# Two layers of convolution and feed-forward with their gradients: w1's gradient made features by rows, in pairs of blocks, with column halves

## The chip, the cores and the metric

One core of one Trainium2 chip. The metric is device time of one launch in microseconds (us), the median of several runs; lower is better. A profile belongs to one execution, whose own time is given beside it. PE is the matrix engine (TensorE), PEld its weight loads, ACT, DVE and POOL are ScalarE, VectorE and GpSimd, and SP is the engine whose queue here only starts DMAs. A matmul multiplies weights that lie in the 128x128 array (`lhsT`, at most 128 rows by 128 columns) by a moving operand (`rhs`, 128 rows by up to 512 columns) and adds into PSUM: one partition for each column of the weights, one column for each column of the moving operand.

## The reference

The forward function is applied to a sequence of 2048 tokens with D = 448 features, and the reference returns its output and the gradients of all inputs and weights but one:

```python
x = A_q
x = x + _A_ref(_layernorm(x), A_k, A_v, A_shift_k, A_ssm_k, A_ssm_D)
x = x + _B_ref(_layernorm(x), B_w1, B_w2)
x = x + _A_ref(_layernorm(x), A_k, A_v, A_shift_k, A_ssm_k, A_ssm_D)
x = x + _B_ref(_layernorm(x), B_w1, B_w2)
```

`_A_ref` is a gated long convolution through an FFT. `_B_ref` is the feed-forward part, with F = 1792:

```python
h = jnp.einsum("bsd,df->bsf", x, w1)
h = _silu(h)
out = jnp.einsum("bsf,fd->bsd", h, w2)
```

Output 7 is the gradient of w1, shape (448, 1792), bfloat16. For each of the two uses of `_B_ref` it is the sum over all tokens of (normalised row of x) times (gradient at h), and the two are added. Output 8, w2's gradient, is a sum of the same kind, shape (1792, 448).

## The kernel before

Tokens lie in 16 tiles of 128 (`NT`), features of the feed-forward part in 14 blocks of 128 (`NF`). The kernel has three stages. A prefix computes spectra and convolutions. `Main.run` goes over four chunks of 512 tokens, forward and backward through both layers; it stores the activations `a` and the gradients `g` at h to device memory (`OP_d`), laid out so that a block of 128 features of all tokens can be loaded as a tile [128 tokens, 16, 128 features] of 512 KB. `_ssm_suffix` then computes the gradients of the convolution.

The gradients of w2 and w1 are made by the class `Jobs`. `Jobs.steps` is a generator that issues the matmuls in order; it stops at each `yield`, and the code around it takes up a few steps with `jobs.run(n)`. The order of TensorE's instructions is the program's (`manual_schedule`), so the jobs' matmuls stand in TensorE's queue exactly where they are woven in: from the last chunk of `Main.run` on, all through the suffix, and what is left at the very end (`jobs.run(1000)`, L1352). One step is four matmuls of 448 columns.

For w1, a call of `group` (L1005) makes one block `f` of 128 features (the last call makes two, 12 and 13). It loads the block's tile of `g` of layer 1 (`load`, L972), takes a PSUM bank (`bank`, L998), and issues 16 matmuls (`mms`, L992), one for each tile of tokens. Then it does the same with layer 0 into the same bank. The weights are `g`'s tile and the moving operand is the normalised row (`n3` for layer 1, `n1` for layer 0, all 448 features), so the sum stands as [128 features of h, 448 features of x], the transpose of what is stored:

```python
self.nc.tensor.matmul(ps[:, :D], lhsT=st[:, t, :], rhs=mov[:, t, :],
                      start=(first and t == 0), stop=(last and t == NT - 1))
```

`fin_w1` (L1102) copies the bank to a tile `dout` on ACT and leaves it pending. The next call of `fin_w1` or `fin_w2` calls `flush` (L1108): four TensorE transposes of 112 features each into the bank `tr` (`ps_dt`, L1117), a copy on ACT to the tile `do7` (L1119), and a DMA from POOL's queue to output 7 (L1120). w2's blocks have their sum as it is stored and need no transposes: `fin_w2` (L1095).

`load` takes its tiles in turn from two pools with three buffers each. All loads go through SP's queue in their order. `bank` takes its tags in turn from po, jb, po; po has two banks, jb and tr one each. `n1` and `go2` (L1079, L1072) load a moving operand at the first call: `n1` over the tile of `go`, `go2` over the tile of `n3`, so each waits until the operand before it has been read.

Elsewhere the kernel uses parts of the array at once. In `_products` (L513) the last 64 of the 448 rows of two blocks lie on the array's upper and lower 64 rows, and their matmuls stand side by side. In the suffix, L1318 multiplies bands of 32 features on four (at the end two) groups of 32 columns, with 128 moving columns:

```python
nc.tensor.matmul(pd[32 * b:32 * b + 32, 0, P * r0:P * r0 + P], lhsT=gks[:, sl_, ch],
                 rhs=kx[:, sl_:sl_ + 4, ch], start=(sl_ == 0), stop=(sl_ == 15))
```

L235 and L236 (inverse transforms) and L1305 are full matmuls of 128 moving columns, each with weights of its own.

Of the kernel before, what the change touches and what calls it, by code (L numbers as in the profile page):

```python
# [11 lines left out]
BF16 = mybir.dt.bfloat16  # L12
# [5 lines left out]
P = 128  # L18
S = 2048
D = 448  # L20
F = 1792
J = 16
NT = 16
DC = 112
ND = 4
NF = 14
# [60 lines left out]
class _Bal:  # L87

    def __init__(self, nc):
        self.nc = nc  # L90
        self.load = {"act": 0.0, "dve": 0.0}
# [446 lines left out]
class Main:  # L538
# [245 lines left out]
    def run(self, es):  # L784
# [27 lines left out]
        def steps(pattern, **gens):  # L812
            for ch in pattern:
                next(gens[ch], None)

        steps("GGtttG", G=g20, t=self.T2(self.n0[0][1], nT))
        gb = gb_load(0)
        weave("H" * 7, H=self.H(0, 0, nT, r, range(14)))
# [7 lines left out]
        gh21 = []  # L826
        g21 = self.G(gT, gh21)
        steps("GGGG", G=g20)
        next(g20, None)
        nT = self.nT()  # L830
        steps("tGtGtGt", G=g21, t=self.T2(self.n1[1], nT))
        r = []
        weave("H" * 7, H=self.H(0, 1, nT, r, (1, 3, 5, 6, 7, 9, 11, 13)))
# [89 lines left out]
class Jobs:  # L923


    def __init__(self, k, main):
        self.k, self.nc, self.main = k, k.nc, main
        self.pool = main.ch
        self.n_ld = self.n_bank = 0
        self.pend = None  # L930
        self.last_ld = None

    def gen(self):
# [71 lines left out]
    def group(self, fts, keys, movs, fin, tags=None):  # L1005
        ps = {}
        tags = tags or [None] * len(fts)
        for i, ft in enumerate(fts):
            st = self.load(keys[0], ft)
            ps[ft] = self.bank(tags[i])  # L1010
            yield from self.mms(ps[ft], st, movs[0](), 0, NT, True, False)
        if fts == (12, 13):
            self.go2()
        for ft in fts:
            st = self.load(keys[1], ft)
            if fts == (5, 6) and ft == 5:
                self.load_n3()
            yield from self.mms(ps[ft], st, movs[1](), 0, NT, False, True)
            fin(ft, ps[ft])
# [17 lines left out]
    def steps(self):  # L1037
        g2 = lambda: self.k.mov2
        go = lambda: self.go
        keys = (("a", 1), ("a", 0))  # L1040
        yield from self.opening()
        yield from self.group((3,), keys, (go, g2), self.fin_w2, tags=("jb",))
        yield from self.group((4,), keys, (go, g2), self.fin_w2, tags=("tr",))
        yield from self.group((5, 6), keys, (go, g2), self.fin_w2)
        wkeys = (("g", 1), ("g", 0))
        movs = (lambda: self.n3, self.n1)
        for f in range(12):
            yield from self.group((f,), wkeys, movs, self.fin_w1)
        yield from self.group((12, 13), wkeys, movs, self.fin_w1)
        for f in range(7, 13):  # L1050
            yield from self.group((f,), keys[::-1], (g2, self.go2), self.fin_w2)
        yield from self.last_block(keys[::-1], (g2, self.go2))

    def last_block(self, keys, movs):

        nc, k = self.nc, self.k
        ft = NF - 1
        o = self.out()
        st = [self.load(key, ft) for key in keys]
        for lo, hi in ((0, 320), (320, D)):  # L1060
            ps = self.bank(None)
            for i in range(2):
                mov = movs[i]()
                for t in range(NT):
                    nc.tensor.matmul(ps[:, lo:hi], lhsT=st[i][:, t, :], rhs=mov[:, t, lo:hi], start=(i == 0 and t == 0), stop=(i == 1 and t == NT - 1))  # L1065
                    if t % 4 == 3:
                        yield 1
            nc.scalar.copy(o[:, lo:hi], ps[:, lo:hi])
            nc.sync.dma_start(out=k.outs[8][ft * P:(ft + 1) * P, lo:hi], in_=o[:, lo:hi])
        self.flush()  # L1070

    def go2(self):  # L1072
        k = self.k
# [21 lines left out]
    def fin_w2(self, ft, ps):  # L1095
        nc, k = self.nc, self.k
        o = self.out()
        nc.scalar.copy(o[:], ps[:, :D])
        self.flush()
        (nc.gpsimd if ft < NF - 2 else nc.sync).dma_start(out=k.outs[8][ft * P:(ft + 1) * P, :], in_=o[:])  # L1100

    def fin_w1(self, ft, ps):  # L1102
        o = self.out()
        self.nc.scalar.copy(o[:], ps[:, :D])
        self.flush()
        self.pend = (ft, o)

    def flush(self):  # L1108
        nc, k = self.nc, self.k
        if self.pend is None:  # L1110
            return
        ft, o = self.pend
        self.pend = None
        out7v = k.outs[7].rearrange("(c p) f -> p c f", p=DC)
        pt = k.psum.tile([DC, ND, P], BF16, name="ps_dt", tag="tr", bufs=1)
        for dc in range(ND):
            nc.tensor.transpose(pt[:, dc, :], o[:, dc * DC:(dc + 1) * DC], k.ident[:])  # L1117
        o7 = k.dp3.tile([DC, ND, P], BF16, name="do7", tag="do7", bufs=2)
        nc.scalar.copy(o7[:], pt[:])  # L1119
        nc.gpsimd.dma_start(out=out7v[:, :, ft * P:(ft + 1) * P], in_=o7[:])  # L1120


class APart:
# [259 lines left out]
```

## Time and profile before

| | |
|---|---|
| time, median of 3 runs | 717.25 us (716.99 to 719.49) |
| time of the profiled execution | 716.31 us |
| its span, first to last instruction | 714.5 us |
| mean granted TensorE clock | 0.995 |
| w1's matmuls (`ps_d<-n3m` and `ps_d<-n1m`) | 448, from 531.9 to 662.8 us |
| w1's transposes (`ps_dt`) | 56, from 549.3 to 672.7 us |
| ACT's copies of w1's sums (L1104), of the transposes (L1119) | 14 of 537 ns, 14 of 601 ns |
| POOL's issues to output 7 (L1120) | 14 of 730 ns |
| landing of a tile `dstat` after its issue | 3.5 to 15.3 us, median 5.7 us |

A line of a group of instructions reads: line of the program, engine, operation, output<-inputs, shapes, count | busy time (the union of the spans) and mean span of one in ns | idle time of the engine before them. A matmul's span includes the time that its results take to leave the array, so spans of a stream of matmuls overlap, and the cost of one is the distance from its start to the next one's. In the chain of waits, each piece is start, length and work; it runs backwards from the last instruction over what released each.

### The profile page before, as it was taken

How to read it: one execution, taken by the hardware profiler on the slowest of the kernel's cores; microseconds unless marked ns; L12 is line 12 of the kernel's file. 1: busy time of each engine (PE TensorE's matmuls, PEld its weight loads, DVE VectorE, ACT ScalarE, POOL GpSimd, SP SyncE). 2: the span in 40 equal slices, each digit the busy share in tenths (PEclk: the TensorE clock that was granted, in tenths of full speed). 3: DMA queues.
4: the chain of work that ended last, by engine and by line, in shares of the span. 5: the costliest groups of instructions: out<-in, count | busy, mean ns of one | idle time of the engine just before them, and what ended most of it. 6: DMA issues, size and time to landing. Idle time of an engine off the chain costs nothing.

```text
span 714.5 us, 12786 instructions
## 1 busy us (share of the span) xinstructions
PE 689.3 (96%) x5008; PEld 380.9 (53%) x5008; DVE 486.2 (68%) x1106; ACT 444.2 (62%) x582; POOL 123.3 (17%) x208
## 2 busy tenths in 40 slices
PE   6997899999999999999999999999999999999998
PEld 4886654434444444444444444544566666656655
DVE  4788776758887747877279723934258769869790
ACT  3878877686777868778677685132755555545200
POOL 1034420111011100111001100001212223353130
PEclk9999899999999999999999999999999999999999
DMA  9949998659969999499975999089999897879962
GB/s 303 305 146 234 342 287 255 168 139 270 236 146 235 215 240 242 116 243 231 224 179 133 233 229 365 3 187 249 309 413 357 291 343 245 266 274 377 354 181 95
DMA packets 196237, 172.59 MB, mean 242 GB/s; under 512 B 143090, under 2 KB 174194, under 8 KB 195024
## 3 DMA queue, kind: packets, MB, share of 16 engines
q1 hardware_dynamic: 181280, 115.30, 61.3%
q0 software_dynamic: 13344, 52.54, 20.9%
q10 hardware_dynamic: 1552, 3.94, 1.5%
q8 instruction: 39, 0.64, 0.4%
q14 instruction: 22, 0.18, 0.1%
HBM read 73.25 MB, written 60.10 MB: 187 GB/s over the span
## 4 chain that ended last, share of the span: by engine, by line
PE 62%; issue 8%; DVE 5%; ACT 4%; DMA 3%; POOL 2%; POOLq 0%; DVEq 0%; ACTq 0%
PE ps_d L995 12%; PE ps_n L741 12%; PE ps_h L513 11%; PE ps_g L513 10%; PE ps_o L695 7%; PE ps_d L1030 3%; ACT dT L688 2%; DMA ksf<-KS_d 1%; PE ps_t L580 1%; PE ps_gK L1305 1%; PE ps_tr L1211 1%; POOL rstd L279 1%; PE ps_d L1065 1%; PE ps_s L206 1%; DVE n L287 1%
## 5 line engine op out<-in xcount | busy, mean ns | idle before, releaser
L995 PEld LDWEIGHTS <-dstat 128*128 128x128 bf16 x768 | 72.5, 98 | 61.1
L513 PE MATMUL ps_h<-nT,w1sb 128*128 128x512 bf16 (+1 forms) x448 | 97.4, 380 | 2.6 <-ACT dT L678 1.9
L741 PE MATMUL ps_n<-w1T,ghT 128*128 128x448 bf16 x448 | 92.5, 353 | 0.8 <-DVE ghT L866 0.8
L695 PE MATMUL ps_o<-w2sb,aT 128*128 128x448 bf16 x448 | 88.5, 352 | 0.0
L513 PE MATMUL ps_g<-nT,w2T 128*128 128x512 bf16 (+1 forms) x392 | 82.9, 380 | 0.1
L723 ACT CAST ghT<-ps_g 128x512 bf16<-128x512 f32 (+1 forms) x74 | 54.1, 760 | 41.5 <-PE ps_g L513 41.2
L673 ACT ACTIVATE aT<-ps_h 128x512 bf16<-128x512 f32 (+1 forms) x82 | 60.0, 759 | 29.2 <-PE ps_h L513 27.6
L513 PEld LDWEIGHTS <-w1sb 128*128 128x128 bf16 (+1 forms) x448 | 35.5, 97 | 59.7 <-issue 25.4
L741 PEld LDWEIGHTS <-ghT 128*128 128x128 bf16 x448 | 43.2, 98 | 42.3 <-DVE ghT L866 1.7
L695 PEld LDWEIGHTS <-aT 128*128 128x128 bf16 x448 | 43.5, 98 | 40.1
L513 PEld LDWEIGHTS <-w2T 128*128 128x128 bf16 (+1 forms) x448 | 35.4, 97 | 55.1 <-issue 20.8
L915 DVE SCALAR_TENSOR_TENSOR lb_v<-lb_u,n 128x448 bf16<-128x448 bf16 x48 | 30.0, 624 | 46.8 <-ACT lb_u L745 46.3
L279 POOL TENSOR_TENSOR rstd<-ln_ve,mhalf 128x2 f32<-128x2 f32 (+2 forms) x27 | 23.0, 851 | 198.8 <-DVE ln_ve L277 198.8
L688 ACT ACTIVATE dT<-dT 128x1024 bf16<-128x1024 bf16 (+1 forms) x64 | 55.0, 940 | 0.1
L995 PE MATMUL ps_d<-n1m,dstat 128*128 128x448 bf16 x224 | 48.6, 352 | 0.0
L995 PE MATMUL ps_d<-n3m,dstat 128*128 128x448 bf16 x224 | 48.6, 352 | 0.0
L678 ACT CAST dT<-ps_h 128x1024 bf16<-128x1024 f32 (+1 forms) x50 | 42.8, 872 | 0.0
L745 ACT ACTIVATE lb_u<-ps_n,rstd 128x448 bf16<-128x448 f32 x32 | 20.7, 647 | 34.5 <-PE ps_n L741 26.3
L995 PE MATMUL ps_d<-X,dstat 128*128 128x448 bf16 x160 | 34.2, 353 | 0.0
L995 PE MATMUL ps_d<-go,dstat 128*128 128x448 bf16 x160 | 33.7, 353 | 0.0
L581 ACT COPY nT<-ps_t 128x1024 bf16<-128x1024 bf16 x20 | 20.2, 1008 | 18.7 <-PE ps_t L580 18.7
L866 DVE TENSOR_TENSOR ghT<-dT,ghT 128x512 bf16<-128x512 bf16 (+2 forms) x24 | 18.1, 778 | 19.2 <-ACT ghT L723 17.0
(217 smaller groups left out, 1245.1 us busy)
## 6 DMA issues: line engine op xcount, KB each, us to landing
dstat<-g_d SPq DMA_DIRECT2D x28, 512.0 KB, 5.6
dstat<-a_d SPq DMA_DIRECT2D x23, 512.0 KB, 7.1
a_d<-turned SPq DMA_DIRECT2D x16, 512.0 KB, 4.1
g_d<-turned SPq DMA_DIRECT2D x16, 512.0 KB, 3.9
a_d<-turned SPq DMA_DIRECT2D x16, 384.0 KB, 3.3
g_d<-turned SPq DMA_DIRECT2D x16, 384.0 KB, 3.3
N_d<-n POOLq DMA_DIRECT2D x10, 448.0 KB, 4.6
spec_K<-ZK POOLq DMA_DIRECT2D x7, 512.0 KB, 7.7
```

What stands on the lines that cost most here:

```text
L279: k.ln_pow = nc.gpsimd.tensor_tensor(out=r[:, lo:hi], in0=ve[:, 0:n], in1=k.mhalf[:, 0:n], op=ALU.pow)
L513: nc.tensor.matmul(ps(u, u + 1)[:, 0, :], lhsT=wT[h, b, ft * P:(ft + 1) * P], rhs=rhs[h, b, :], start=start, stop=stop)
L673: self.last_silu = nc.scalar.activation(aT[hh][:, o:o + hi - lo, :], ps(lo, hi), ACT.Silu)
L678: nc.scalar.copy(self.dpart(dT, 2 * fp + lo, 2 * fp + hi), ps(lo, hi))
L688: self.nc.scalar.activation(d[:, o:o + n, :], d[:, o:o + n, :], ACT.Derivative_silu)
L695: nc.tensor.matmul(po[:, :D], lhsT=aT[ft // 7][:, ft % 7, tl * P:(tl + 1) * P], rhs=self.w2sb[:, ft, :], start=(ft == 0), stop=(ft == NF - 1))
L723: nc.scalar.copy(g, ps(lo, hi))
L741: nc.tensor.matmul(pn[:, :D], lhsT=gh[ft // 7][:, ft % 7, tl * P:(tl + 1) * P], rhs=self.w1T[:, ft, :], start=(ft == 0), stop=(ft == NF - 1))
L745: nc.scalar.activation(u0[:], pn[:, :D], ACT.Identity, scale=k.rstd[2 * L + 1][:, t:t + 1], accum_out=cp[:, tl, 0:1])
L915: nc.vector.scalar_tensor_tensor(out=v[:], in0=u0, scalar=-1.0 / D, in1=n_t, op0=ALU.mult, op1=ALU.mult, accum_out=cp[:, 1:2])
L995: self.nc.tensor.matmul(ps[:, :D], lhsT=st[:, t, :], rhs=mov[:, t, :], start=(first and t == 0), stop=(last and t == NT - 1))
L1030: nc.tensor.matmul(ps[ft][:, :D], lhsT=get(t), rhs=mov[:, t, :], start=ft not in seen, stop=(last[ft] == i and t == hi - 1))
```

## The change

The gradient of w1 is made by a new function, `pair`, for two blocks at a time. Weights and moving operand change places: the normalised row gives the weights, 128 features of it at a time, and `g`'s tile is the moving operand, 128 columns. The sum stands as [features of x, features of h], as it is stored. The 448 features are three full groups of 128 and a rest of 64. The rests of the two blocks go to columns 0 to 63 and 64 to 127 of the array, and their sums to the two halves of the partitions of columns 384 to 511 of the first block's bank. Transposes, `flush` and the pending tile are gone. A step of the generator is now two tiles of tokens of one layer for both blocks (16 matmuls); a pair has 16 steps, as two blocks had before. The banks are po and po for even pairs, jb and tr for odd ones. ACT copies 512 columns of the first bank and 384 of the second; each block is stored by two DMAs, of 384 and 64 rows. `go2` is called after layer 1 of the last pair.

```diff
         wkeys = (("g", 1), ("g", 0))
         movs = (lambda: self.n3, self.n1)
-        for f in range(12):
-            yield from self.group((f,), wkeys, movs, self.fin_w1)
-        yield from self.group((12, 13), wkeys, movs, self.fin_w1)
+        for i in range(NF // 2):
+            yield from self.pair(i, wkeys, movs)
...
-    def fin_w1(self, ft, ps):
-        o = self.out()
-        self.nc.scalar.copy(o[:], ps[:, :D])
-        self.flush()
-        self.pend = (ft, o)
-
-    def flush(self):
+    def pair(self, i, keys, movs):
+
         nc, k = self.nc, self.k
-        if self.pend is None:
-            return
-        ft, o = self.pend
-        self.pend = None
-        out7v = k.outs[7].rearrange("(c p) f -> p c f", p=DC)
-        pt = k.psum.tile([DC, ND, P], BF16, name="ps_dt", tag="tr", bufs=1)
-        for dc in range(ND):
-            nc.tensor.transpose(pt[:, dc, :], o[:, dc * DC:(dc + 1) * DC], k.ident[:])
-        o7 = k.dp3.tile([DC, ND, P], BF16, name="do7", tag="do7", bufs=2)
-        nc.scalar.copy(o7[:], pt[:])
-        nc.gpsimd.dma_start(out=out7v[:, :, ft * P:(ft + 1) * P], in_=o7[:])
+        fts = (2 * i, 2 * i + 1)
+        ps = [self.bank(tag) for tag in (("jb", "tr") if i % 2 else ("po", "po"))]
+        for L in range(2):
+            st = [self.load(keys[L], ft) for ft in fts]
+            n = movs[L]()
+            for t in range(NT):
+
+                last = L == 1 and t == NT - 1
+                for b in range(3):
+                    cols = slice(b * P, (b + 1) * P)
+                    for u in range(2):
+                        nc.tensor.matmul(ps[u][:, cols], lhsT=n[:, t, cols], rhs=st[u][:, t, :], start=(L == 0 and t == 0 and b == 0), stop=(last and b == 2))
+                    if b == 0:
+                        for u in range(2):
+                            nc.tensor.matmul(ps[0][64 * u:64 * u + 64, 384:512], lhsT=n[:, t, 384:D], rhs=st[u][:, t, :], start=False, stop=False)
+                if t % 2:
+                    yield 1
+            if L == 0 and i == NF // 2 - 1:
+                self.go2()
+        out = k.outs[7]
+        for u, ft in enumerate(fts):
+            o = k.dp3.tile([P, 4, P], BF16, name="dout", tag="do7", bufs=2)
+            if u == 0:
+                o0 = o
+            m = 4 - u
+            nc.scalar.copy(o[:, 0:m, :], ps[u][:, 0:m * P].rearrange("p (b f) -> p b f", f=P))
+            cols = slice(ft * P, (ft + 1) * P)
+            nc.gpsimd.dma_start(out=out[0:384, cols].rearrange("(b p) f -> p b f", p=P), in_=o[:, 0:3, :])
+            nc.gpsimd.dma_start(out=out[384:D, cols], in_=o0[64 * u:64 * u + 64, 3, :])
```

The calls of `flush` in `last_block` and `fin_w2` are removed as well.

More of the change, by code (lines that the diff above doesn't have):

```diff
@@ L1011, in group @@
             yield from self.mms(ps[ft], st, movs[0](), 0, NT, True, False)
-        if fts == (12, 13):
-            self.go2()
         for ft in fts:
@@ L1098, in fin_w2 @@
         nc.scalar.copy(o[:], ps[:, :D])
-        self.flush()
         (nc.gpsimd if ft < NF - 2 else nc.sync).dma_start(out=k.outs[8][ft * P:(ft + 1) * P, :], in_=o[:])
-    def fin_w1(self, ft, ps):
-        o = self.out()
-        self.nc.scalar.copy(o[:], ps[:, :D])
-        self.flush()
-        self.pend = (ft, o)
-    def flush(self):
-        nc, k = self.nc, self.k
-        if self.pend is None:
-            return
-        ft, o = self.pend
-        self.pend = None
-        out7v = k.outs[7].rearrange("(c p) f -> p c f", p=DC)
-        pt = k.psum.tile([DC, ND, P], BF16, name="ps_dt", tag="tr", bufs=1)
-        for dc in range(ND):
-            nc.tensor.transpose(pt[:, dc, :], o[:, dc * DC:(dc + 1) * DC], k.ident[:])
-        o7 = k.dp3.tile([DC, ND, P], BF16, name="do7", tag="do7", bufs=2)
-        nc.scalar.copy(o7[:], pt[:])
-        nc.gpsimd.dma_start(out=out7v[:, :, ft * P:(ft + 1) * P], in_=o7[:])
+    def pair(self, i, keys, movs):
+        nc, k = self.nc, self.k
+        fts = (2 * i, 2 * i + 1)
[26 more added lines that the diff above has]
+            nc.gpsimd.dma_start(out=out[384:D, cols], in_=o0[64 * u:64 * u + 64, 3, :])
```

## The prediction

> **What bounds the kernel now.** The profiled execution took 716.31 us: a span of 714.5 us and 1.8 us around it. I read the page first, then the windows of the stretch in which w1's gradient is made, then the chain of waits there.
>
> ```profile
> PE 689.3 (96%) x5008; PEld 380.9 (53%) x5008; DVE 486.2 (68%) x1106; ACT 444.2 (62%) x582; POOL 123.3 (17%) x208
> ```
>
> PE is the one full engine, but 96% is an average, and a busy PE may be a badly used one. So the windows (width, then busy time and instructions of each engine, clock, DMA share, GB/s). The first is split where w1's products begin:
>
> ```profile
> 531.00:600.00 69.00, 69.00 (x596) 44.34 (x594) 53.44 (x121) 38.32 (x45) 19.81 (x35) 1.00 0.90 326
> 600.00:640.00 40.00, 40.00 (x337) 25.37 (x336) 28.95 (x75) 18.76 (x23) 15.71 (x25) 1.00 0.76 248
> 640.00:678.00 38.00, 37.92 (x506) 24.79 (x504) 32.80 (x43) 16.89 (x25) 9.38 (x17) 1.00 0.98 376
> 678.00:712.00 34.00, 33.57 (x212) 19.01 (x208) 18.69 (x32) 3.88 (x8) 7.48 (x13) 1.00 0.50 148
> ```
>
> From 531 us to the end PE never rests: 69.00 of 69.00, 40.00 of 40.00, then 37.92 of 38.00. The granted clock is 1.00 throughout, and the list of waits of PE from 531 us on is empty. TensorE's order is fixed by the program, so each job's matmuls stand between the suffix's, and what comes later comes later by all that is added. This stretch has no spare PE time in which longer products could hide. DVE at 53 of 69 us and POOL at 20 of 69 us have spare time.
>
> The groups of instructions between 531 and 678 us give the parts that the change touches (count | union of their spans, mean span of one | idle before). The mean span is latency, since matmuls are pipelined:
>
> ```profile
> L995 PE MATMUL ps_d<-n1m,dstat 128*128 128x448 bf16 x224 | 48.6, 352 | 0.0
> L995 PE MATMUL ps_d<-n3m,dstat 128*128 128x448 bf16 x224 | 48.6, 352 | 0.0
> L1117 PE MATMUL ps_dt<-ident,dout 128*112 128x128 bf16 x56 | 5.4, 219 | 0.0
> L1318 PE MATMUL ps_sk<-kx_s,gks 128*32 128x128 bf16 x224 | 4.3, 220 | 0.0
> ```
>
> What one costs in a stream is read from the chain of waits (start, length, what), which runs from matmul to matmul:
>
> ```profile
> 540.01 2.27 PE ps_d L995 x12
> ...
> 664.12 0.89 PE ps_gK L1305 x16
> 665.02 1.51 PE ps_d L995 x8
> ...
> 673.71 1.01 PE ps_sk L1318 x64
> 674.72 2.38 PE ps_d L995 x12
> 677.09 1.00 PE ps_sk L1318 x32
> 678.09 27.35 PE ps_d L995 x144
> ```
>
> - 448 columns: 1.51 / 8 = 189 ns (2.27 / 12 as well).
> - 128 columns with new weights each time: 0.90 us to the next piece / 16 = 55.8 ns. The 98 ns span of a weight load is hidden behind the matmul before it.
> - Column bands: L1318 uses 32 columns of the array at a time. Four bands side by side (64 instructions, 16 sets) take 1.01 us, two (32, also 16 sets) take 1.00 us. So matmuls on different columns run at once, and two cost one slot.
> - But 16 slots should be 16 x 55.8 = 893 ns, not 1000: 107 ns more. And the 12 matmuls behind the bands take 2.38 us where 12 take 2.27 elsewhere: 110 ns more. One visit to column bands costs **0.217 us** beside its work.
>
> The timeline shows where:
>
> ```profile
> 676.55 0.54 PE L995 MATMUL ps_d<-X,dstat 128*128 128x448 bf16 x2
> 677.02 0.23 PE L1318 MATMUL ps_sk<-kx_s,gks 128*32 128x128 bf16 x2
> ```
>
> The second of the two full matmuls starts 189 ns after 676.55, at 676.74; a next full one would start at 676.93, the first band starts at 677.02. Some 90 ns of the array pass with nothing new entering, and about as much on the way back.
>
> The kernel's other tiled matmuls, halves of 64 rows in L513, agree:
>
> ```profile
> 205.46 11.43 PE ps_g L513 x56
> 334.62 1.73 PE ps_g L513 x8
> ```
>
> A full 512-column matmul is 1.73 / 8 = 216 ns. The 56 are 44 full ones and 12 halves, two at once: 50 slots, 10.81 us. The other 0.62 us falls on three visits: **0.207 us** each. Two widths, rows and columns, give the same price within 10 ns.
>
> **The change, part by part.**
>
> *The products.* Before, two blocks at one step t of one layer are 2 x 189 = 378 ns. After, they are six full matmuls of 128 columns and two on 64 columns of the array each. The order is b=0 twice, the two halves, b=1 twice, b=2 twice: the halves stand alone between full ones, at every t. That is 7 slots (the halves share one) x 55.8 = 390.6 ns, and one visit to column mode. I take 0.212 us for it, the middle of 0.207 and 0.217: 602.6 ns, 224.6 more. There are 7 pairs x 2 layers x 16 steps = 224 of these, so +50.3 us.
>
> The bounds of a visit: 64-column halves stand nowhere in the trace. Below, only one of its two edges might cost (0.107 us; the nearest rows always show both). Above, the 112-column weight loads have a span of 130 ns against 97 for 32 columns, so 64 columns may take some 13 ns more than the bands' load (an estimate, linear between these two), and that load isn't hidden: 13 x 224 = +2.9 us. A free visit is the rival below. For the middle value I allow 185 to 240 ns, so 50.3 less 6 or plus 6.
>
> By the Trainium skill, TensorEngine Tiling (Array Packing), "Theoretical Speedup", a dimension of up to 64 gives up to twice the speed; by that alone the halves would share a slot and the sum would be 716 us. Its "Key Properties" say that a change of tiling mode drains the array; the 0.207 and 0.217 us agree, and the page has no price.
>
> *The transposes.* 14 x 4 at 55.8 ns go: -3.1 us, all on PE's path (they stand between PE's matmuls without a gap).
>
> *Evacuation.* Per block, ACT did a copy of 448 (537 ns) and one of the transposed 512 (601 ns). Now it does one copy of 512 or 384. ACT is busy 38 of 69 us, and is not what PE waits for: 0, hidden behind matmuls; without that cover some 7 us of ACT at most.
>
> *Stores.* Per block one POOL issue of 730 ns becomes two, of 0.55 to 0.73 us (other POOL issues take 542): 14 more issues, some 7 us of POOL, which has 100 of 147 us free. They wait for the copy at the end of a pair; behind them in POOL's queue stand the loads q_g, q_n, q_y and spectra. The suffix reaches these later by the same stretch that PE adds. Two rather than one store at a time wait there, for about a copy (0.5 to 0.8 us): 0.
>
> *Loads.* The same 28 tiles of 512 KB through the same six buffers, now freed two at a time. A step over one layer of a pair lasts at least 16 x 0.6 = 9.6 us, and two such steps cover the landing (3.5 to 15.3 us). n1m is asked for two loads later and used four yields later; go2 has 9.6 us of pair 6 where it had 6. SP's queue waits for PE, not PE for it: 0.
>
> *Banks.* Pairs use po+po and jb+tr in turn, so a copy has a whole pair's time. Only the last pair (po, po) is followed by a group that asks for a po bank: PE may wait for one copy, 0 to 1 us. I take 0.4, since suffix matmuls (0.89 us of ps_gK) often stand between two runs of jobs.
>
> *Sum:* 50.3 - 3.1 + 0.4 = +47.6, and 716.3 + 47.6 = **764 us**. The median of the runs is 0.9 us above the profiled one, inside what follows.
>
> **Rivals.**
> 1. *The halves' weights load behind the full matmuls, as full weights do, and a visit is free.* Then 390.6 - 378 = 12.6 ns x 224 = 2.8, -3.1, +0.4: 716 us, not slower. It decides at 16 ns: below that per visit the end is within 0.5%. For it: nothing but that 64 columns weren't seen. Against it: 0.207 and 0.217 in two other shapes. One edge free is the half-way case: 107 ns, 740 us.
> 2. *The two halves don't run at once* (both add into one bank, in different partitions): +55.8 x 224 = 12.5, 777 us. Against it: two bands of L1318 into one bank cost one slot.
> 3. *128-column matmuls can't be kept up for 10 us.* The trace has them in bursts of 16 to 64. Its slowest row at full clock, L235 and L236 of the prefix, is 14.9 us for 208: 72 ns. Then 7 x 71.6 + 212 - 378 = 335 ns x 224 = 75, in all 789 us. Against it: that row is cut up by waits for DVE. The Trainium skill, TensorE: Matmul & The Clock Gate, "Back-to-back issue gap", gives about 81 ns as what is sustained at 128 columns; by it 803 us. The 55.8 ns bursts of this trace don't show it.
>
> **How the numbers follow.** The sum 0.77 (its own range 757 to 771); halves in turn 0.07; free visits 0.05; one edge 0.04; slow stream 0.04; other things (a clock that drops as the array drains, a late load) 0.03. The range 756 to 779 takes in the sum and the halves in turn and leaves out 16 in 100. This kernel's runs tell 0.5%, 3.6 us, from no change. Only free visits could end within that (0.04) or a little below (0.01); slower is 0.95.
>
> **What would show it.** In the trace after, 64-column matmuls should start some 95 ns after their slot, in pairs 3 ns apart, and the full one behind them as late; a period of t at 0.60 us, the pairs' matmuls in all 135 us against 85. No ps_dt, no idle of PE for banks or loads over 1 us, clock 1.00. The last groups of w2 should be as now, 48 us later. A period of 0.39 or 0.66 us, or PE waiting on dstat, would prove me wrong.

## The result, and the profile after

| | before | after |
|---|---|---|
| median of 4 runs each | 717.12 us (712.58 to 719.49) | 765.11 us (764.51 to 765.96) |
| ratio of the means | | 1.068, 95% interval 1.062 to 1.073 |
| profiled execution, span | 716.31, 714.5 us | 764.79, 763.0 us |
| w1's first matmul to the end of the span | 531.9 to 714.5: 182.6 us | 529.4 to 763.0: 233.6 us |

The kernel became slower by 48.0 us, or 6.7%, by the medians; 764 us were forecast. The last row is the steadiest measure: it was 182.6, 182.9 and 183.0 us in three profiles of the kernel before, and 233.6 both times in two of the changed one. It is called "the stage" below. By it the change costs 51 us. The 3 us between 51 and 48 lie ahead of the stage, and are taken up in "The stretch ahead of the stage" and under "The total".

The page's first part and the windows of the changed kernel, from w1's first matmul on (width, then busy time and instructions of each engine, clock, DMA share, GB/s):

```profile
PE 732.4 (96%) x6252; PEld 430.5 (56%) x6296; DVE 487.5 (64%) x1106; ACT 437.3 (57%) x568; POOL 131.6 (17%) x222
```

```profile
529.00:600.00 71.00, 70.74 (x941) 53.46 (x943) 42.00 (x92) 26.45 (x29) 19.12 (x33) 1.00 0.74 266
600.00:660.00 60.00, 59.89 (x821) 46.15 (x822) 34.44 (x83) 19.99 (x23) 15.64 (x27) 1.00 0.51 168
660.00:711.00 51.00, 51.00 (x657) 37.72 (x655) 35.87 (x58) 17.68 (x22) 16.14 (x27) 1.00 0.80 291
711.00:760.00 49.00, 48.38 (x504) 28.27 (x504) 22.23 (x36) 6.34 (x13) 9.91 (x17) 1.00 0.53 163
```

PE is as "busy" as before, 96%, and the clock is 1.00. Nothing in these lines says that for over a third of each step (0.227 of 0.617 us, worked out below) no new matmul takes its slot: the span of a matmul is 0.22 us or more where its slot is 0.056, so spans overlap and cover such a gap. ACT lost 7 us and DVE nothing. What the share of busy time hides, the chain of waits shows (start, length, what):

```profile
688.05 0.44 PE ps_d L1110 x6
688.50 0.18 PE ps_d L1113 x2
688.67 0.33 PE ps_d L1110 x4
689.00 0.89 PE ps_gK L1312 x16
```

Sixteen full matmuls of the suffix take 0.89 us, 55.8 ns each, and the four of w1's ahead of them take 0.33 us with what leads back into full mode. Six of w1's that stand between two visits take 0.44 us where 6 x 55.8 is 0.335, and a pair of halves takes 0.18 us where a slot is 0.056. Both edges cost, 0.12 and 0.11 us. The timeline of two steps (start, length from first start to last end, what) gives the period:

```profile
599.89 0.25 PE L1113 MATMUL ps_d<-dstat,n1m 128*64 128x128 bf16 x2
600.07 0.51 PE L1110 MATMUL ps_d<-dstat,n1m 128*128 128x128 bf16 x6
600.50 0.25 PE L1113 MATMUL ps_d<-dstat,n1m 128*64 128x128 bf16 x2
600.68 0.51 PE L1110 MATMUL ps_d<-dstat,n1m 128*128 128x128 bf16 x6
601.12 0.25 PE L1113 MATMUL ps_d<-dstat,n1m 128*64 128x128 bf16 x2
```

From pair to pair of halves: 601.12 - 599.89 = 1.23 us for two steps, 0.617 us each (0.603 in the sum). From the start of the last full matmul before a visit to the start of the second one behind it, the median over all 224 visits is 394.0 ns; the three slots in between take 167.5, so a visit costs **226.5 ns** (0.212 in the sum).

The weight loads of the first of these steps show where the time goes:

```profile
599.88 0.11 PEld L1113 LDWEIGHTS <-n1m 128*64 128x64 bf16 x2
600.06 0.34 PEld L1110 LDWEIGHTS <-n1m 128*128 128x128 bf16 x6
```

Within a run of full matmuls a load starts some 54 ns before its own matmul and so lies behind the one before it. At both edges the first load starts only 2 to 4 ns before its matmul (599.88 and 599.89, 600.06 and 600.07). Nothing new starts in the 147 ns from the start of the last full matmul to the halves' load, nor in the 172 ns between the second half and the full load behind it. Whether the array is empty by then the trace doesn't show: the halves start 149 ns after the last full matmul, whose modelled span is 219 ns.

Of the groups of instructions between 529 and 712 us, two more lines, the halves of layer 0 and the one wait that PE got, for the bank behind the last pair (ps_dt is in no group any more):

```profile
L1113 PE MATMUL ps_d<-dstat,n1m 128*64 128x128 bf16 x224 | 27.6, 243 | 0.0
...
L994 PE MATMUL ps_d<-X,dstat 128*128 128x448 bf16 x1 | 0.3, 349 | 0.6 <-ACT dout L1124 0.6
```

### The profile page after: what moved, and what is told of

It reads as the page before. It is cut to its first block, busy times and chain, and to the rows that moved or that the text cites. A ratio compares the mean times of both kernels' runs of the same rounds, so it can differ in the third digit from the quotient of the medians.

```text
span 763.0 us, 15313 instructions
## 1 busy us (share of the span) xinstructions
PE 732.4 (96%) x6252; PEld 430.5 (56%) x6296; DVE 487.5 (64%) x1106; ACT 437.3 (57%) x568; POOL 131.6 (17%) x222
## 4 chain that ended last, share of the span: by engine, by line
PE 73%; issue 3%; DVE 3%; DMA 3%; ACT 3%; POOL 1%; SPq 0%; POOLq 0%
PE ps_d L1110 13%; PE ps_n L741 11%; PE ps_h L513 10%; PE ps_g L513 10%; PE ps_o L695 8%; PE ps_d L994 6%; PE ps_d L1113 5%; PE ps_d L1027 2%; DMA dstat<-a_d 2%; PE ps_v L236 2%; PE ps_v L235 2%; PE ps_t L580 1%; PE ps_gK L1312 1%; DMA turned<-ghT 1%; POOL rstd L279 1%
## 5 line engine op out<-in xcount | busy, mean ns | idle before, releaser
L513 PE MATMUL ps_h<-nT,w1sb 128*128 128x512 bf16 (+1 forms) x434 | 95.7, 380 | 3.5 <-ACT dT L678 1.9
L513 PE MATMUL ps_g<-nT,w2T 128*128 128x512 bf16 (+1 forms) x378 | 81.2, 380 | 1.1 <-issue 0.5
L1110 PE MATMUL ps_d<-dstat,n3m 128*128 128x128 bf16 x672 | 62.7, 221 | 0.3
L1110 PE MATMUL ps_d<-dstat,n1m 128*128 128x128 bf16 x672 | 62.0, 221 | 0.1
L994 PEld LDWEIGHTS <-dstat 128*128 128x128 bf16 x320 | 30.6, 98 | 30.3 <-DMA dstat<-a_d 2.1
L1110 PEld LDWEIGHTS <-n3m 128*128 128x128 bf16 x672 | 39.8, 98 | 10.7
L1110 PEld LDWEIGHTS <-n1m 128*128 128x128 bf16 x672 | 39.4, 98 | 9.2
L111 ACT CAST B1v<-ps_v 128x1024 bf16<-128x1024 f32 x14 | 14.2, 1012 | 45.5 <-PE ps_v L236 45.5
```

Source lines behind the costliest of these rows:

```text
L513: nc.tensor.matmul(ps(u, u + 1)[:, 0, :], lhsT=wT[h, b, ft * P:(ft + 1) * P], rhs=rhs[h, b, :], start=start, stop=stop)
L1110: nc.tensor.matmul(ps[u][:, cols], lhsT=n[:, t, cols], rhs=st[u][:, t, :], start=(L == 0 and t == 0 and b == 0), stop=(last and b == 2))
```

## The experiments

Theory A: the price is one of *visits*. Every time that the array goes from full matmuls to column halves and back, 0.227 us pass, whatever is done there. The rivals: B, the 64-column matmuls themselves are dear, wherever they stand; C, long streams of 128-column matmuls are slow. Numbers from w1's first matmul to the end are "stage" again.

### Halves of two steps together

```diff
-                    if b == 0:
-                        for u in range(2):
-                            (half u of step t)
+                if t % 2:
+                    for t in (t - 1, t):
+                        for u in range(2):
+                            (half u of step t)
                 for b in range(3):
...
```

> The halves of two steps of tokens stand together: 112 visits to column mode instead of 224, the same matmuls. Theory A (a price of 0.227 us for each visit, whatever is done in it): 112 x 0.227 = 25.4 us less than the change, about 740 us. Theory B (the price lies in the 64-column matmuls themselves, 0.283 us for each pair of halves, wherever they stand): no difference, 765 us. Theory C (the price is that of streams of 128-column matmuls, not of the halves): 765 us.

741.47 us (2 runs); the stage 208.9 us, 24.7 below the change's. The chain of waits:

```profile
640.64 0.34 PE ps_d L1113 x6
640.98 0.23 PE ps_d L1109 x4
641.21 0.78 PE ps_d L1113 x12
641.99 0.23 PE ps_d L1109 x4
```

In this kernel L1109 is the halves, L1113 the full ones. Four halves, two slots, take 0.23 us: twice the work of a visit, and still 0.12 us over its slots. The twelve full ones behind take 0.78 against 0.67. The same matmuls with half the visits save half the price: B and C fall.

### Halves of one layer of a pair together

The same edit with `if t == NT - 1: for t in range(NT)`, so that 32 halves stand together.

> All halves of one layer of a pair stand together: 14 visits instead of 224, the same matmuls. Theory A (0.227 us for each visit): 210 x 0.227 = 47.7 us less, about 717 us, as the kernel before. Theories B (each pair of halves has its price) and C (128-column streams are slow): 765 us.

721.19 us (10 runs), 1.005 times the kernel before (1.002 to 1.007) on the same chip; the stage 188.4 us. A visit with 32 halves in it costs 227.1 ns by the median, one with four 227.7, one with two 226.5: the price doesn't depend on what is done there. The chain shows such a visit:

```profile
655.62 0.34 PE ps_d L1113 x6
655.96 1.01 PE ps_d L1109 x32
656.97 1.11 PE ps_d L1113 x18
```

32 halves are 16 slots, 0.893 us, and 0.12 over; 18 full ones 1.005, and 0.11 over. A's 717 us were 4 too low. By the profiles 2.5 us of that lie in the stage (188.4 where 233.6 less 47.7 is 185.9), and the rest ahead of it (w1's first matmul began at 531.0 us, 1.6 later than in the changed kernel). The list of PE's waits (total, times, longest, in us) has 2.0 of the 2.5:

```profile
PE ps_gkv L1292 <- ACT gkv L1294: 2.0, 1, 2.0
PE ps_d L994 <- ACT dout L1124: 0.6, 1, 0.6
```

The second line is the bank, 0.6 us as in the changed kernel. The first is new there: the suffix is now waited for. More on that below.

### No column mode at all

```diff
-                for b in range(3):
-                    cols = slice(b * P, (b + 1) * P)
+                for b in range(4):
+                    lo = min(b * P, D - P)
                     for u in range(2):
-                        (weights n[:, t, cols], bank columns cols)
+                        (weights n[:, t, lo:lo + P], bank columns b * P to (b + 1) * P)
```

> No column halves: the last weights are features 320 to 447, 128 of them, for each block, of which the upper 64 are stored. Eight full matmuls for each step. Theory A: 8 x 55.8 = 446 ns where a step now takes 618, so 172 x 224 = 38.5 us less, about 727 us, although there are more column steps. Theory B: the same. Theory C (a 128-column matmul costs over 72 ns in a long stream): 8 x 72 = 576 ns, 755 us or more.

727.89 us (4 runs), 1.016 times the kernel before (1.012 to 1.020); the stage 196.4 us, 37.2 below the change's. It streams eight slots of 128 columns a step where the change has seven, and is 37 us faster. A row of 22 of them took 1.39 us from the first start to the last end; less 0.22, the span of the last one, that is 1.17 / 21 = 55.7 ns. The stage as a whole says the same: 182.6 + 224 x (446.4 - 378.4) ns - 3.1 + 0.8 is 195.5 us, and at 72 ns it would be 29 us more. C is excluded.

### The two halves apart

The first half stands behind b = 0, the second behind b = 1.

> The two halves of a step stand apart, with full matmuls between them: 448 visits of one half each. Theory A: 224 more visits at 0.227 us and 224 more slots at 0.056 us, 63 us more, about 828 us. Theory B (0.14 us for each half): 765 us. If only a slot is lost: 777 us.

826.44 us (2 runs); the stage 295.4 us, 61.8 above the change's. A visit with one half in it costs 223.5 ns by the median. B falls from this side as well.

### One half only

> Only the first block's half is computed and stored; rows 384 to 447 of output 7 are missing for odd blocks. As many visits, with one matmul in each. If the two halves share a slot, as the sum took it: no difference, 765 us and 618 ns a step. If they run one after the other: 0.056 x 224 = 12.5 us less, 752 us.

767.29 us (one run); the stage 232.9 us, 0.7 less than the change's. (w1's first matmul began at 532.5 us in it, 3.1 later, which is the rest.) The second half costs 3 ns a step: the halves share their slot.

### Halves of 32 columns

> The halves have 32 columns each instead of 64 (rows 416 to 447 of output 7 are left out), on the same places of the array. If the 15 ns by which a visit came out dearer than in the sum (227 against 212) are the longer load of 64 columns that nothing hides: 212 to 217 ns a visit, 2 to 3.5 us less, about 762 us. If not: 227 ns, 765 us.

762.23 us (one run); the stage 230.7 us, 2.9 less. The timeline:

```profile
600.16 0.23 PE L1113 MATMUL ps_d<-dstat,n1m 128*32 128x128 bf16 x2
600.32 0.51 PE L1110 MATMUL ps_d<-dstat,n1m 128*128 128x128 bf16 x6
600.76 0.23 PE L1113 MATMUL ps_d<-dstat,n1m 128*32 128x128 bf16 x2
```

The full ones now start 0.16 us behind the pair (0.18 before), and a step takes 0.60. By the median a visit costs 212.5 ns, near the 217 that the bands of L1318 had shown in the kernel before. So the 14 ns more come with the width of the halves. Their weight loads differ by as much, 106 ns for 64 columns and 92 for 32; that the load is what is waited for is argued from these equal figures.

### The halves left out

> The halves are left out, so output 7 lacks its last 64 rows. Theory A: each step loses a visit and a slot, 0.283 us x 224 = 63 us less, about 702 us, the step at 6 x 55.8 = 335 ns. Theory C (slow 128-column streams): 6 x 72 = 432 ns, about 723 us.

724.28 us (one run), 22 more than A's 702. The stage is 187.5 us where 233.6 less 63.3 is 170.3. PE's work did shrink as expected: w1's matmuls stand 55.8 ns apart. But PE now waits. From the list of waits of all engines:

```profile
DVE q_y L1151 <- DMA q_y<-Y_d: 19.0, 5, 9.7
...
ACT gkv L1288 <- DVE gks L1291: 8.1, 1, 8.1
...
PE ps_gkv L1286 <- ACT gkv L1288: 5.2, 1, 5.2
...
DVE gks L1291 <- DMA gks<-in_A_v_dram: 4.6, 1, 4.6
...
PE ps_v L235 <- DVE pa L1242: 4.3, 1, 4.3
```

The columns are the total, the times and the longest, in us. DVE stands up to 9.7 us before the loads q_y of the part that makes output 1 (`APart`), and the products pa, for which PE waits, stand behind that in DVE's queue. The other long wait goes back over ACT's copy gkv and DVE to the load gks, which POOL issues behind APart's loads. PE's waits for other engines and for loads come to 11.7 us, with 0.3 of its own issue 12.0. The other 5 us are in these windows:

```profile
595.00:601.00 6.00, 5.38 (x52) 5.20 (x53) 5.88 (x14) 1.01 (x1) 3.79 (x7) 0.53 0.94 286
...
646.00:655.00 9.00, 7.95 (x73) 5.75 (x73) 6.93 (x12) 5.41 (x8) 1.08 (x2) 0.68 1.01 386
```

At the end of each of the two pauses (4.3 us until 595.0, 5.2 until 647.1) the granted clock falls to 0.5 for 6.8 us (from 593.8 and from 645.0 us); 0.53 and 0.68 are the means of the windows. PE has work in some 10 us of that, and half of it, some 5 us, is lost. So theory F was formed: right behind PE's chain lies a second one, through APart's loads and DVE's queue, and time that is taken from PE in this stage comes back as waits.

### The halves and APart left out

`APart.run` returns at once.

> As the kernel without the halves (rows 384 to 447 of output 7 left out), and also without the part of the suffix that makes output 1 (APart's loop: its loads q_g, q_n, q_y, its DVE work and its stores). Theory F (the 17 us that the kernel without halves did not gain were waits for this part, which goes through POOL's loads and DVE's queue): PE's gaps of 15 us shrink to under 5, the stage from w1's first matmul to the end falls from 187.5 to 171 to 175 us, some 705 to 710 us in all. If the waits come from elsewhere in the suffix: 187 us still.

707.74 us (one run); the stage is 171.0 us, where the sum says 170.3, and PE's list of waits has 1.1 us in all. F holds: the 17 us were waits for this part and for what stands behind it in the queues, some 12 us, and the low clock that came with them, some 5 us. That both its loads and its DVE work are gone here leaves open which of the two was the tighter. The trace of the kernel without the halves speaks for the loads: DVE stood 19.0 us before q_y there, and POOL, which issues these loads, stood before q_g until a store of output 1 had landed (total, times, longest):

```profile
POOL q_g L1137 <- DMA out_dram<-q_g: 43.6, 6, 14.1
```

### One visit for a pair

The kernel of 14 visits, with the halves of layer 1 behind its full matmuls and those of layer 0 right after them, 7 visits in all, and bank jb for the group behind the last pair:

```diff
+                if L == 1 and t == 0:
+                    (both halves of all 16 steps)
                 for b in range(3):
                     (full matmuls as before)
+                if L == 0 and t == NT - 1:
+                    (both halves of all 16 steps)
...
+        self.n_bank += 2
         for f in range(7, 13):
```

The `yield`s move with the halves, so that all 64 of a pair stand in one step of the generator, which lasts some 3 us where most others last 0.67.

> One visit for each pair (the halves of layer 1 behind its full matmuls, those of layer 0 right after them), 7 in all, and bank jb for the group of w2 that follows the last pair. Theory A (a visit is 0.227 us, the bank 0.78): from w1's first matmul to the end, 182.7 + 2.7 (390.6 against 378.4 ns a step) - 3.1 (transposes) + 7 x 0.227 = 184 us if PE stays the bound, 4 less than with 14 visits (188.4), 717 us in all. Theory F (behind PE stands a second chain, the suffix's own loads and DVE, which ends just before it): the time saved comes back as waits of ps_gkv and ps_v, and the stage stays at 185 to 188 us, 717 to 721 us in all: no better than the kernel before.

720.13 us (12 runs, 716.89 to 726.21), 1.007 times the kernel before (1.004 to 1.009) on the same chip. Theory A's 184 us don't come, as F said, but F missed as well: the stage is 191.7 us, above its 185 to 188 (the total lies in its 717 to 721). The list of PE's waits is

```profile
PE ps_v L236 <- DVE pb L1254: 2.8, 2, 2.0
PE ps_gkv L1297 <- ACT gkv L1299: 1.4, 1, 1.4
PE ps_d L994 <- issue: 1.0, 1, 1.0
PE ps_v L235 <- ACT Zg L1241: 0.4, 1, 0.4
```

5.6 us, among them the waits of ps_gkv and ps_v that F had named. PE's work is 184 us by the sum, and a granted clock of 0.5 from 622.0 to 625.4 us, behind the wait of 2.0, took up to 1.7 more: 191.3 in all. Whether the waits are those of the second chain alone, or come in part of the one long step of each pair, was not tested apart. The wait for the bank is gone. No complete version with the new form of the sums came out faster than the kernel before: without any visit it would save 0.4 us of PE's work by the sum (+2.7 - 3.1), and the 7 visits alone cost 1.6.

### The stretch ahead of the stage

Two more profiles of the kernel before, one more of the changed one.

> The kernel before, once more with a profile, for its stage from the first of w1's matmuls to the end and for where its first job begins. Theory D (the 4.4 us by which the changed kernel's first job began earlier, 439.3 against 443.7 us, is chance of the execution): the first job begins anywhere between 439 and 446 us, and the stage from w1's first matmul to the end takes 182.6 us within 0.5. Theory E (the change itself moves the earlier stages): 443.7 us within 0.5.

> The kernel before, a third profile, for where w1's first matmul begins (531.9 and 532.0 us in the two so far; 528.2 to 531.0 in the six changed versions on the other chip, with the same instructions up to there). Theory D (chance of the execution): anywhere between 528 and 535 us. Theory E (the changed versions reach this point some 2.5 us earlier): 531.5 to 533 us. The stage behind it 182.6 to 183 us in both.

> The changed kernel, a second profile, for where w1's first matmul begins (529.4 us in the first). Theory D (chance): anywhere between 528 and 535 us. Theory E (earlier than in the kernel before): 528.5 to 530.5 us. The stage behind it 233.6 us within 0.5 in both.

716.75, 722.50 and 765.10 us. The first job began at 443.7, 442.3 and 441.2 us in the kernel before, at 439.3 and 441.5 in the changed one. w1's first matmul began at 531.9, 532.0 and 537.7 us in the kernel before, at 529.4 and 529.7 in the changed one, and at 528.2 to 535.0 in the versions of it, though PE's matmuls up to there are the same. The stages were 182.9, 183.0 and 233.6 us. 537.7 lies outside what either theory gave, and its profile says why: PE stood for the load of a block of `a` (for w2's gradient),

```profile
PE ps_d L995 <- DMA dstat<-a_d: 6.5, 1, 6.5
```

and the granted clock was 0.5 from 520.4 to 527.2 us. So the stretch varies by several us from one execution to the next, which is D as far as it goes. Whether the new form reaches the stage earlier on the mean, five profiles can't tell. The medians of the runs speak for it: the changed kernel lies 48.0 us above the kernel before, where its stage is 50.8 longer than the mean of 182.8; for the four versions that were run beside the kernel before on one chip, in the order above, it is 24.0 against 26.1, 3.7 against 5.5, 10.4 against 13.6 and 109.0 against 112.6. All five are short by 2 to 4 us, but most of these differences lie within the intervals of the runs, and why it should be so stays open.

## Why the prediction was right

**What bounds the kernel.** Right. PE had no spare time in the stage, and 224 x (7 x 55.8 + 226.5 - 378) = +53.6 us, less 3.1 for the transposes and with 0.8 for the bank, is 51.3 us; the stage grew by 51.0.

**The slots.** Right: seven slots of 55.8 ns. The halves share one (the kernel with one half), and a long stream keeps 55.8 (the kernel without column mode).

**The price of a visit.** This is the mechanism of the forecast, and grouping shows it: 448, 224, 112 and 14 visits gave stages of 295.4, 233.6, 208.9 and 188.4 us, with the same halves in each. The size was a little low: 212 was taken, 226.5 measured, 3.2 us in all. The prediction's upper bound named the reason, a wider weight load that nothing hides (13 ns by a line through other widths); halves of 32 columns cost 14 ns less, and their loads took 14 ns less. So the step that was mis-sized is the width: the prediction held that two widths give the same price within 10 ns, but its columns were 32 wide and its 64 were rows. The Trainium skill, TensorEngine Tiling (Array Packing), "Key Properties", cited in the prediction, says that a change of tiling mode drains the array. The four stages above agree as far as the price goes with the number of changes. The Trainium skill's "Theoretical Speedup" on the same page, up to two for 64 columns, holds here for the slot alone (3 ns for the second half).

**Transposes, evacuation, stores, loads.** Right as far as can be seen: ps_dt is gone, and ACT's 7 us less and POOL's 14 issues more moved nothing. PE's list of waits in the stage has the bank alone.

**The bank.** 0.4 was taken, 0.78 us is the gap (the list of waits has 0.6 of it).

**The total.** The sum of these was 3.4 us too low for the stage, and w1's first matmul began 2.5 us earlier in the profiled execution than in the one of before, which hid most of it. The prediction had no term for that, so by luck 764 came nearer to 765.1 than its terms deserve.

**The rivals.** Free visits (716 us), one edge only, halves in turn and a slow stream are all excluded, by the chain and by the kernels above. What the prediction did not see is what would have come of a cheaper visit: it put "716 us" for free visits, and the two kernels with nearly none ended at 720 to 721, in part for the 14 and 7 visits that are left (3.2 and 1.6 us), in part since PE then waits for the suffix (2.0 and 5.6 us). The chain of waits of the kernel before had hinted at it, with long pieces of DMA on the way to an end that PE reached without waiting:

```profile
572.82 9.18 DMA ksf<-KS_d
603.05 2.54 DMA q_g<-G_d
621.77 5.07 DMA q_y<-Y_d
634.97 5.22 DMA gks<-in_A_v_dram
```

So two chains run side by side there. In the other two profiles of the kernel before PE did wait in the stage, 0.4 and 0.5 us, each time for the same copy gkv as in the kernels with few visits.

## What to carry to other kernels

Count how often the array changes between full and partial tiles, not how much is done in each: one trip there and back cost 0.21 to 0.23 us here, as much as four full matmuls of 128 columns, and grouping the partial ones cut the bill from 224 trips to 14. A busy share doesn't show such gaps; the distance between starts does. And before work is taken from the engine that bounds a stretch, look for the second chain: here it lay within a few us, and of the 63 us that leaving the halves out took from PE's work, 17 came back as waits and low clock.

## What the runs showed of the hardware

A pause of the matrix engine can cost more than itself. At the end of 4.3 and of 5.2 us without matmuls the granted clock fell to 0.5 for 6.8 us, so that the kernel without the halves lost some 5 us of its gain to the clock; in the kernel of one visit for a pair a wait of 2.0 us was followed by 3.4 us at 0.5 (a mean of 0.78 between 618 and 625 us); without the pauses (APart left out) it stayed at 1.00 for the whole stage. Not every pause did this: one of 2.0 us in the kernel of 14 visits and one of 3.1 us ahead of the stage in the kernel without the halves were followed by none.
